# Sliding-window attention and an ELU feed-forward on one core: the order of the first four steps and of the last two products

## The chip, the core and the metric

The kernel runs on one core of a Trainium2 chip. A core has five engines that work side by side, each with an instruction queue of its own that it takes strictly in order, and wait for each other through semaphores: TensorE (PE in the profile; its weight loads are a row of their own, PEld), VectorE (DVE), ScalarE (ACT), GpSimd (POOL) and SyncE (SP). Data come from and go to the main memory by DMA, issued here from the queues of SP, ACT and POOL. Products of PE go to PSUM, and DVE or ACT take them from there into the core's working memory.

The metric is the time of one execution in microseconds (us) on the device. Lower is better.

## The reference: what is computed

Attention with a symmetric window over 8 batches, 8 heads, 576 positions and a head width of 64, and a feed-forward network on its result (4608 tokens by 512, 2048 hidden, ELU):

```
mask   = |pos_i - pos_j| <= 32
attn   = softmax(where(mask, q @ k.T / 8, -1e9))
x      = (attn @ v), heads side by side      # 4608 x 512
h      = x @ w_in                            # 4608 x 2048
g      = where(h > 0, h, exp(min(h, 0)) - 1)
out    = g @ w_out                           # 4608 x 512, float32
```

The inputs are float32; the products run in bfloat16 with float32 sums.

## The kernel before

**Attention.** Queries are taken in blocks of 64, two blocks (a pair) at a time; 36 pairs in all. For a pair, `scores` (L297) makes the transposed scores in PSUM, `exponential` (L312) takes them through ACT, `mask` (L319) multiplies by 0 and 1 on DVE, `pv` (L328) multiplies by the values and by a column of ones that gives the sums, `normalize` (L342) divides on DVE (a reciprocal and a product), `x_transpose` (L353) turns the result on PE and `x_evac` (L369) copies it to `xT`. A block of 64 queries needs 128 keys that start 32 before it. So values are loaded in two forms: `V_e[b]` holds blocks m of 128 positions that start at 128 m - 32, by `load_v` (L138), and `V_o[b]` holds the same rows shifted by 64, made from `V_e` by two copies of half the partitions each: `rotate_v` (L150) on DVE. Part 0 reads blocks m0 to m1 of `V_e`, part 1 the blocks one further on. Pairs 2 and 3 (blocks 4 to 7 of the first batch) use blocks 2 to 4 of the values, and so wait for the loads of values 3 and 4.

**Feed-forward.** Tokens go in tiles of 256 (two pairs), 18 tiles. The hidden width is worked in 8 steps of 256 columns per tile, 144 steps `kk`. A step is: the first product `mm1(kk)` (L591, 8 matmuls of 128x256 into PSUM `h0` or `h1` in turn), exp on ACT (e_sb), minus 1 (m_sb; on DVE, or on ACT for steps 1 to 3), `elu(kk)` (L623, one operation on DVE that joins the two cases and frees the PSUM tile), and the second product `mm2(kk)` (L635, 4 matmuls of 128x512: 2 halves of 128 rows by 2 blocks of the hidden width) that adds into the tile's output in PSUM. The first product of a step needs the tile's `xT` (both pairs); `order` (L586) makes steps 0 to 3 the first half of tile 0, steps 4 to 7 the first half of tile 1 (pairs 2 and 3), and then the second halves.

**Order.** It is written out by hand (`manual_schedule`): each engine gets its instructions in the order of the code. The loop at L661 runs for each kk: slot "first", `elu(kk-1)`, slot "dve", `mm1(kk)`, slot "mid", the due `mm2`, slot "end". `at(kk, slot, fn, ...)` puts pieces of attention into the slots. `mm2` follows two steps behind `mm1`, except at the start, where a small table delays products 0 to 3, and at the end, where 142 and 143 come after the last `mm1`. `idle(n, tag)` puts n matmuls on zeros into PE's queue.

The start, step by step: steps 0 and 1 need the first quarter of w_in, steps 2 and 3 the second, products 0 and 1 the first quarter of w_out. POOL's queue loads, with a cast to bfloat16: values 1, 0, 2; the second half of the first batch's q and k (`load_cast`); `load_w_in(0)`; three small operations on masks; `load_w_in(1)`; values 3 and 4; `load_w_out(0)` and `(1)`; then the next batch and the rest of the weights. Pairs 2 and 3 have scores and exponential behind step 0, masks around step 1, and rotation, `pv`, normalization and transpose in step 3, with products 0 and 1 between.

The end: `mm2(143)` is followed by two copies of 128x512 from PSUM, the first half's on DVE (written out from SP's queue), the last half's on ACT (from ACT's queue).

Of the kernel before, what the change touches and what calls it, by code (L numbers as in the profile page):

```python
# [9 lines left out]
FP32 = mybir.dt.float32  # L10
# [11 lines left out]
def kernel(  # L22
# [9 lines left out]
    nc = tc.nc  # L32
# [5 lines left out]
    D_MODEL = H * D  # L38
# [8 lines left out]
    VS = 5  # L47
# [7 lines left out]
    STEPS = NFO // FG  # L55
    HALF = STEPS // 2
    NSTEP = NT * STEPS
# [9 lines left out]
    opool = ctx.enter_context(tc.tile_pool(name="outs", bufs=2))  # L67
# [26 lines left out]
    def ps_tile(shape, dt, tag, name):  # L94
        return pools[tag].tile(shape, dt, tag=tag, name=name)
# [42 lines left out]
    def load_v(b, m):  # L138
        lo = 128 * m - WIN
        p0 = max(0, -lo)  # L140
        p1 = min(128, S - lo)
        nc.gpsimd.dma_start(  # L142
            out=V_e[b % 3][p0:p1, m, :, 0:D],
            in_=v[b, :, lo + p0:lo + p1, :].rearrange("h p d -> p h d"))
# [28 lines left out]
    def load_w_in(c):  # L173
        w = D_FF // 4
        nc.gpsimd.dma_start(  # L175
            out=w_in_sb[:, :, c * w:(c + 1) * w],
            in_=moe_w_in[:, c * w:(c + 1) * w].rearrange(
                "(o p) f -> p o f", p=128))

    def load_w_out(c):  # L180
        n = NFO // 4
        nc.gpsimd.dma_start(
            out=w_out_sb[:, c * n:(c + 1) * n, :],
            in_=moe_w_out[c * n * 128:(c + 1) * n * 128, :].rearrange(
                "(o p) f -> p o f", p=128))
# [46 lines left out]
    def copy_on(eng, d_, s_):  # L232
        if eng is nc.scalar:
            nc.scalar.copy(d_, s_)  # L234
        else:
            eng.tensor_copy(d_, s_)  # L236
# [169 lines left out]
    for mi in (0, 4):  # L406
# [4 lines left out]
        out=masks[:, 3, :], in_=masks[:, 3, :], compare_op=ALU.is_ge,  # L411
        fill=0.0, base=128 - WIN - 1, pattern=[[0, QB]],
        channel_multiplier=-1)
    load_w_in(1)
    for m in (3, 4):
        load_v(0, m)
    load_w_out(0)
    load_w_out(1)

# [49 lines left out]
    def at(kk, slot, fn, *args):  # L469
        tasks.setdefault((kk, slot), []).append((fn, args))  # L470

    def run(kk, slot):
        for fn, args in tasks.get((kk, slot), ()):
            fn(*args)
# [11 lines left out]
    at(0, "mid", scores, 3, "u")  # L486
    for i in (2, 3):
        at(0, "mid", exponential, i)
        at(1, "dve" if i == 2 else "mid", mask, i)
        at(3, "dve", rotate_v, 0, 2, VS - 1, (i - 2,))  # L490
        at(3, "mid", pv, i)

    at(1, "mid", idle, 3, "y1")
    at(3, "dve", idle, 3, "y1")
    for i in (2, 3):
        at(3, "mid", normalize, i)
    at(3, "mid", lambda: elu(2))
    for i in (2, 3):
        at(3, "mid", lambda n: mm2(n), i - 2)
        at(3, "mid", x_transpose, i)  # L500
        at(3, "mid", x_evac, i, nc.scalar)
    at(4, "dve", swap_pools)

    for part, kq in ((HALF_A, 7), (HALF_B, 15)):
# [20 lines left out]
    for i in range(4, NPAIR):  # L525
        two = i >= FIRST_TWO
        kk, z = begin[i], i % 2 if two else 0
# [5 lines left out]
        n = kk + (3 + z if two else 2)  # L533
# [55 lines left out]
    psH, m_t, g_t, psY = {}, {}, {}, {}  # L589

    def mm1(kk):  # L591
        t, s = order[kk]
        h = kk % 2


        tags = (f"h{h}", "s") if kk == NSTEP - 1 else (f"h{h}",)
        w = FG // len(tags)
        psH[kk], m_t[kk] = [], []
        for z, tag in enumerate(tags):
            ps = ps_tile([128, w, TT], FP32, tag, "ps")  # L600
            psH[kk].append(ps)
            for j in range(w):
                fo = s * FG + z * w + j
                for do in range(NDO):
                    nc.tensor.matmul(  # L605
                        ps[:, j, :],
                        lhsT=w_in_sb[:, do, fo * 128:(fo + 1) * 128],
                        rhs=xT[t][:, :, do, :],
                        start=(do == 0), stop=(do == NDO - 1))
        for z, ps in enumerate(psH[kk]):  # L610
            e_sb = mpool.tile([128, w, TT], FP32, tag="e_sb", name="e_sb")
            nc.scalar.activation(e_sb, ps, AX.Exp)  # L612
            m_sb = mpool.tile([128, w, TT], BF16, tag="m_sb", name="m_sb")
            if 1 <= kk <= 3:

                nc.scalar.activation(m_sb, e_sb, AX.Copy, bias=-1.0)
            else:
                nc.vector.tensor_scalar(m_sb, e_sb, -1.0, None, ALU.add)  # L618
            m_t[kk].append(m_sb)
            if kk == NSTEP - 1:  # L620
                elu(kk, z)

    def elu(kk, z=0):  # L623
        if z == 0:
            g_t[kk] = mpool.tile([128, FG, TT], BF16, tag="g_sb", name="g_sb",
                                   bufs=5)
        ps = psH[kk][z]
        w = ps.shape[1]
        nc.vector.scalar_tensor_tensor(  # L629
            g_t[kk][:, z * w:(z + 1) * w, :], ps, 0.0, m_t[kk][z],  # L630
            ALU.max, ALU.min)

    out_t = out.rearrange("(t ts p) c -> t p ts c", p=128, ts=TT // 128)

    def mm2(kk):  # L635
        t, s = order[kk]
        if s == 0:
            psY[t] = [ps_tile([128, D_MODEL], FP32, g, "psY")
                      for g in (("h2", "t0") if t == 1 else ("y0", "y1"))]
        g_sb = g_t.pop(kk)  # L640
        last = t == NT - 1 and s == STEPS - 1
        for ts in range(2):
            for j in range(FG):
                nc.tensor.matmul(  # L644
                    psY[t][ts],
                    lhsT=g_sb[:, j, ts * 128:(ts + 1) * 128],
                    rhs=w_out_sb[:, s * FG + j, :],
                    start=(s == 0 and j == 0),
                    stop=(s == STEPS - 1 and j == FG - 1))
        if s == STEPS - 1:  # L650
            for ts in range(2):
                z = 1 - ts if last else ts
                eng = (nc.scalar, nc.vector)[z]
                y_sb = opool.tile([128, D_MODEL], FP32, tag=f"y_sb{z}",
                                  name="y_sb")
                copy_on(eng, y_sb, psY[t][ts])
                (nc.scalar if last and ts else nc.sync).dma_start(
                    out_t[t, :, ts, :], y_sb)

    LAG = 2  # L660
    for kk in range(NSTEP + LAG):  # L661
        run(kk, "first")
        if 1 <= kk < NSTEP and kk != 3:
            elu(kk - 1)
        run(kk, "dve")
        if kk < NSTEP:
            mm1(kk)
        run(kk, "mid")

        for n in {2: (), 3: (), 4: (), 5: (2, 3)}.get(  # L670
                kk, (kk - LAG,) if kk >= LAG else ()):
            mm2(n)
        run(kk, "end")


# [28 lines left out]
```

## Time and profile before

| what | value |
|---|---|
| time, median of 3 runs (lowest, highest) | 306.71 us (306.45, 306.94) |
| the profiled execution: its time, its span | 306.45 us, 304.7 us |
| mean granted clock of TensorE | 1.000 |
| busy: PE, DVE, ACT, POOL | 294.7, 240.7, 170.3, 48.7 us |
| first products, L605: 1152 matmuls | 149.3 us, 273 ns each |
| second products, L644: 576 matmuls | 147.5 us, 379 ns each |
| starts of steps 0, 1, 2, 3, 4 on PE | 15.24, 16.80, 18.54, 20.69, 25.42 us |
| last matmul ends, last copy ends | about 300.40, 301.01 us |

The span runs from the first to the last instruction of the profiled execution; the time of the same execution is 1.75 us longer. A line of the timeline gives start and length in us, the engine, the line of the kernel (that of a helper, where one records the operation), the operation with what it writes and reads and the shape of one, how many are merged into the line, and in brackets how long the engine sat idle ahead of it and what ended that. Matmuls are pipelined: one is listed longer than the time after which the next starts. Line 236 is a copy or cast on DVE, 234 on ACT, whatever it copies. The view of windows gives, for stretches of time, the busy time of each engine, the granted clock, the mean busy share of the 16 DMA engines and the rate in GB/s.

### The profile page before, as it was taken

Reading aid. Unit: us, or ns where it says so; the run is one execution under the profiler, and the core shown is the slowest. Engines: PE = TensorE matmul, PEld = TensorE weight load, DVE = VectorE, ACT = ScalarE, POOL = GpSimd, SP = SyncE. Lnnn points to the kernel's source line nnn. Section 1 sums busy time; section 2 is a strip of 40 time slices with the busy share of each in tenths; the row PEclk is TensorE's granted clock in tenths of the full one; section 3 lists DMA queues with packets and bytes.
Section 4 is the critical chain, followed back from the end, with each engine's and each line's share of the span. In section 5 each row is a group of like instructions: output and inputs, shape, how many; then the busy total and the mean of one; then the engine's idle time right before and its main releaser. Section 6 shows DMA issues by size and latency. Waiting matters only on the chain.

```text
span 304.7 us, 7633 instructions
## 1 busy us (share of the span) xinstructions
PE 294.7 (97%) x3090; PEld 197.0 (65%) x3090; DVE 240.7 (79%) x470; ACT 170.3 (56%) x256; POOL 48.7 (16%) x68
## 2 busy tenths in 40 slices
PE   7799999999999999999999999999999999999994
PEld 3466666677666666666666666666666666666662
DVE  6866587978788887988798879887988787877663
ACT  3673556778664567546754675467545454543431
POOL 8836100910004100230023002300000000000000
PEclk9999999999999999999999999999999999999999
DMA  9999999999766997999799969996911111121011
GB/s 192 189 193 206 182 268 397 309 154 207 167 187 154 297 120 208 225 325 152 154 265 309 183 161 267 321 160 150 269 34 71 34 71 34 72 37 69 8 63 70
DMA packets 91973, 52.81 MB, mean 173 GB/s; under 512 B 76578, under 2 KB 81698, under 8 KB 91938
## 3 DMA queue, kind: packets, MB, share of 16 engines
q1 hardware_dynamic: 47186, 35.48, 43.6%
q0 software_dynamic: 42880, 10.10, 43.2%
q10 hardware_dynamic: 1872, 6.75, 5.7%
q8 instruction: 24, 0.39, 0.5%
q14 instruction: 11, 0.09, 0.1%
HBM read 36.70 MB, written 15.34 MB: 171 GB/s over the span
## 4 chain that ended last, share of the span: by engine, by line
PE 89%; DMA 4%; POOL 3%; DVE 1%; ACT 1%; issue 0%; POOLq 0%; DVEq 0%
PE psY L644 41%; PE ps L605 40%; DMA w_out_sb<-in_moe_w_out_dram 4%; PE psS L336 3%; PE psS L304 3%; POOL Ve L142 1%; PE ptx L279 1%; POOL c L136 1%; PE psXT L357 1%; POOL w_in_sb L175 0%; PE ptx L274 0%; ACT pu L315 0%; DVE x_st L348 0%; DVE pm L324 0%; DVE g_sb L629 0%
## 5 line engine op out<-in xcount | busy, mean ns | idle before, releaser
L612 ACT ACTIVATE e_sb<-ps 128x512 f32<-128x512 f32 (+1 forms) x145 | 86.3, 595 | 118.0 <-PE ps L605 110.4
L605 PE MATMUL ps<-xT,w_in_sb 128*128 128x256 bf16 x1152 | 149.3, 273 | 1.8 <-ACT xT L234 0.7
L644 PE MATMUL psY<-w_out_sb,g_sb 128*128 128x512 bf16 x576 | 147.5, 379 | 0.0
L605 PEld LDWEIGHTS <-w_in_sb 128*128 128x128 bf16 x1152 | 110.5, 98 | 40.7 <-DMA w_in_sb<-in_moe_w_in_dram 1.6
L629 DVE SCALAR_TENSOR_TENSOR g_sb<-ps,m_sb 128x512 bf16<-128x512 f32 (+1 forms) x145 | 99.4, 686 | 13.3 <-DVE m_sb L618 0.5
L618 DVE TENSOR_SCALAR m_sb<-e_sb 128x512 bf16<-128x512 f32 (+1 forms) x142 | 61.2, 431 | 38.3 <-ACT e_sb L612 36.4
L644 PEld LDWEIGHTS <-g_sb 128*128 128x128 bf16 x576 | 54.5, 98 | 38.5 <-DVE g_sb L629 0.2
L142 POOL DMA_DIRECT2D Ve<-in_v_dram x40 | 35.3, 893 | 138.9 <-PE psS L336 79.9
L315 ACT ACTIVATE pu<-psS 128x1024 bf16<-128x1024 f32 x36 | 36.5, 1021 | 1.4 <-PE psS L304 1.4
L348 DVE TENSOR_TENSOR x_st<-psS,rc 128x512 bf16<-128x512 f32 x36 | 24.9, 691 | 1.2
L324 DVE TENSOR_TENSOR pm<-pu,masks 128x1024 bf16<-128x1024 bf16 x36 | 24.6, 683 | 0.7 <-ACT pu L315 0.6
L234 ACT CAST qkb<-f 128x768 bf16<-128x768 f32 (+1 forms) x29 | 24.9, 860 | 0.0
L336 PEld LDWEIGHTS <-pm 128*64 128x64 bf16 x576 | 11.0, 111 | 8.8 <-DVE pm L324 7.7
L336 PE MATMUL psS<-Ve,pm 128*64 128x65 bf16 x320 | 13.2, 196 | 0.8 <-DVE pm L324 0.7
L236 DVE COPY y_sb<-psY 128x512 f32<-128x512 f32 x18 | 12.3, 684 | 0.9 <-PE psY L644 0.9
L304 PEld LDWEIGHTS <-kT 64*128 64x128 bf16 x576 | 9.6, 95 | 4.9 <-issue 4.0
L304 PE MATMUL psS<-qT,kT 64*128 64x64 bf16 x576 | 11.8, 191 | 0.5 <-DVE kT L236 0.5
L336 PE MATMUL psS<-Vo,pm 128*64 128x65 bf16 x256 | 11.9, 196 | 0.0
L234 ACT COPY y_sb<-psY 128x512 f32<-128x512 f32 x18 | 10.5, 582 | 2.2 <-PE psY L644 2.2
L153 DVE COPY Vo<-Ve 64x1040 bf16<-64x1040 bf16 x24 | 10.4, 435 | 1.3 <-DMA Ve<-in_v_dram 0.5
L395 PE MATMUL ps_idle<-zeros 128*128 128x512 bf16 x26 | 8.3, 450 | 1.3 <-DVE zeros L194 1.3
L234 ACT COPY qT<-ptx 128x1152 bf16<-128x1152 bf16 (+2 forms) x8 | 7.5, 972 | 3.5 <-PE ptx L279 2.8
(36 smaller groups left out, 73.3 us busy)
## 6 DMA issues: line engine op xcount, KB each, us to landing
out_dram<-y_sb SPq DMA_DIRECT2D x35, 256.0 KB, 3.7
f<-in_q_dram SPq DMA_DIRECT2D x12, 576.0 KB, 6.1
f<-in_k_dram SPq DMA_DIRECT2D x12, 576.0 KB, 8.2
in_dram<-qkb ACTq DMA_DIRECT2D x10, 576.0 KB, 4.5
Ve<-in_v_dram POOLq DMA_DIRECT2D x24, 128.0 KB, 11.4
w_in_sb<-in_moe_w_in_dram POOLq DMA_DIRECT2D x4, 512.0 KB, 9.8
w_out_sb<-in_moe_w_out_dram POOLq DMA_DIRECT2D x4, 512.0 KB, 12.5
Ve<-in_v_dram POOLq DMA_DIRECT2D x16, 96.0 KB, 10.3
```

The source lines that it names most:

```text
L142: nc.gpsimd.dma_start(out=V_e[b % 3][p0:p1, m, :, 0:D], in_=v[b, :, lo + p0:lo + p1, :].rearrange("h p d -> p h d"))
L234: nc.scalar.copy(d_, s_)
L304: nc.tensor.matmul(psS[:, h % 2, hp * 128 + z * QB:hp * 128 + (z + 1) * QB], lhsT=kT[b % 2][base:base + 64, KPAD + hp * S + QB * qb - WIN: ...
L315: nc.scalar.activation(pu, _bap(psS, [psS.ap[0], [1, 1024]]), AX.Exp, scale=SCALE)
L324: nc.vector.tensor_mul(pm, pu, _bap(mm, [mm.ap[0], [0, H], [1, 2 * QB]]))
L336: nc.tensor.matmul(psS[QB * z:QB * (z + 1), par, hp * VD:(hp + 1) * VD], lhsT=pm[:, par * HP + hp, z * QB:(z + 1) * QB], rhs=vv[:, qb // 2 ...
L348: nc.vector.tensor_mul(x_st, _bap(psS, [psS.ap[0], [VD, HP], [512, 2], [1, D]]), _bap(rc, [rc.ap[0], [2, HP], [1, 2], [0, D]]))
L605: nc.tensor.matmul(ps[:, j, :], lhsT=w_in_sb[:, do, fo * 128:(fo + 1) * 128], rhs=xT[t][:, :, do, :], start=(do == 0), stop=(do == NDO - 1))
L612: nc.scalar.activation(e_sb, ps, AX.Exp)
L618: nc.vector.tensor_scalar(m_sb, e_sb, -1.0, None, ALU.add)
L629: nc.vector.scalar_tensor_tensor(g_t[kk][:, z * w:(z + 1) * w, :], ps, 0.0, m_t[kk][z], ALU.max, ALU.min)
L644: nc.tensor.matmul(psY[t][ts], lhsT=g_sb[:, j, ts * 128:(ts + 1) * 128], rhs=w_out_sb[:, s * FG + j, :], start=(s == 0 and j == 0), stop=( ...
```

## The change

Three things are changed.

1. *Loads.* Values 3 and 4 stand ahead of w_in's second quarter in POOL's queue.
2. *Steps 0 to 3.* Rotations and masks of pairs 2 and 3 follow step 0 (rotation of part 0, mask 2, rotation of part 1, mask 3); both `pv` follow step 1, with 4, 2 and 1 idle matmuls around them (7, in place of 6 in two places); the normalizations stand ahead of step 2; the transposes follow step 3, with `elu(2)` in its usual place at the head of step 3, and products 0 and 1 behind both transposes. Minus 1 of steps 2 and 3 is on DVE.
3. *The end.* Products 142 and 143 run by halves of the rows: 142 and 143 on the first half, then both on the last. The first half is copied by DVE and sent by SP as before. The last half is copied by DVE and ACT, 256 columns each, and sent by SP and ACT.

```
-    load_w_in(1)
     for m in (3, 4):
         load_v(0, m)
+    load_w_in(1)
...
     for i in (2, 3):
         at(0, "mid", exponential, i)
-        at(1, "dve" if i == 2 else "mid", mask, i)
-        at(3, "dve", rotate_v, 0, 2, VS - 1, (i - 2,))
-        at(3, "mid", pv, i)
-
-    at(1, "mid", idle, 3, "y1")
-    at(3, "dve", idle, 3, "y1")
     for i in (2, 3):
-        at(3, "mid", normalize, i)
-    at(3, "mid", lambda: elu(2))
-    for i in (2, 3):
-        at(3, "mid", lambda n: mm2(n), i - 2)
+        at(0, "mid", rotate_v, 0, 2, VS - 1, (i - 2,))
+        at(0, "mid", mask, i)
+
+        at(1, "mid", idle, (4, 2)[i - 2], "y1")
+        at(1, "mid", pv, i)
+        at(2, "dve", normalize, i)
         at(3, "mid", x_transpose, i)
         at(3, "mid", x_evac, i, nc.scalar)
+    at(1, "end", idle, 1, "y1")
     at(4, "dve", swap_pools)
...
-            if 1 <= kk <= 3:
+            if kk == 1:
                 nc.scalar.activation(m_sb, e_sb, AX.Copy, bias=-1.0)
...
-    def mm2(kk):
+    def mm2(kk, parts=(0, 1)):
...
-        for ts in range(2):
+        for ts in parts:
             for j in range(FG):
                 nc.tensor.matmul(
                     psY[t][ts],
-                    lhsT=g_sb[:, j, ts * 128:(ts + 1) * 128],
+                    lhsT=g_t[kk][:, j, ts * 128:(ts + 1) * 128],
...
+        if last and s == STEPS - 1:
+            for ts in parts:
+                for z in range(1 + ts):
+                    c = slice(z * D_MODEL // 2 * ts,
+                              D_MODEL if z == ts else D_MODEL // 2)
+                    eng = (nc.vector, nc.scalar)[z]
+                    y_sb = opool.tile([128, D_MODEL], FP32,
+                                      tag=f"y_sb{1 - z}", name="y_sb")
+                    copy_on(eng, y_sb[:, c], psY[t][ts][:, c])
+                    (nc.scalar if z else nc.sync).dma_start(
+                        out_t[t, :, ts, c], y_sb[:, c])
...
-        if 1 <= kk < NSTEP and kk != 3:
+        if 1 <= kk < NSTEP:
             elu(kk - 1)
...
-        for n in {2: (), 3: (), 4: (), 5: (2, 3)}.get(
+        for n in {2: (), 3: (0, 1), 4: (), 5: (2, 3)}.get(
                 kk, (kk - LAG,) if kk >= LAG else ()):
-            mm2(n)
+            if n < NSTEP - 2:
+                mm2(n)
+            elif n == NSTEP - 1:
+                for ts in range(2):
+                    for m in (n - 1, n):
+                        mm2(m, (ts,))
```

More of the change, by code (lines that the diff above doesn't have):

```diff
@@ L639, in mm2 @@
                       for g in (("h2", "t0") if t == 1 else ("y0", "y1"))]
-        g_sb = g_t.pop(kk)
         last = t == NT - 1 and s == STEPS - 1
-        for ts in range(2):
+        for ts in parts:
             for j in range(FG):
@@ L649, in mm2 @@
                     stop=(s == STEPS - 1 and j == FG - 1))
-        if s == STEPS - 1:
+        if last and s == STEPS - 1:
[9 more added lines that the diff above has]
+                        out_t[t, :, ts, c], y_sb[:, c])
+        elif s == STEPS - 1:
             for ts in range(2):
-                z = 1 - ts if last else ts
-                eng = (nc.scalar, nc.vector)[z]
-                y_sb = opool.tile([128, D_MODEL], FP32, tag=f"y_sb{z}",
+                eng = (nc.scalar, nc.vector)[ts]
+                y_sb = opool.tile([128, D_MODEL], FP32, tag=f"y_sb{ts}",
                                   name="y_sb")
                 copy_on(eng, y_sb, psY[t][ts])
-                (nc.scalar if last and ts else nc.sync).dma_start(
-                    out_t[t, :, ts, :], y_sb)
+                nc.sync.dma_start(out_t[t, :, ts, :], y_sb)
     LAG = 2
```

## The prediction

> **What bounds the kernel now.** I read the page first: its engine table and the chain.
>
> ```profile
> PE 294.7 (97%) x3090; PEld 197.0 (65%) x3090; DVE 240.7 (79%) x470; ACT 170.3 (56%) x256; POOL 48.7 (16%) x68
> ...
> PE 89%; DMA 4%; POOL 3%; DVE 1%; ACT 1%; issue 0%; POOLq 0%; DVEq 0%
> ```
>
> TensorE (PE) is busy 97% of the span and is 89% of the chain. In the view of waits, PE's matmuls from 25 us on wait 0.7 us (for xT, at 25.42) and 0.2 us; its weight loads wait 6.5 us for pm, mostly while earlier matmuls still run. So from step 4 on PE runs almost without gaps, and a change earns time in two places only: ahead of step 4, where the chain is on DMA and POOL, and behind the last matmul. Whatever moves the start of step 4 moves everything behind it.
>
> Second view, the timeline of the first steps (start, length, engine, what ended the idle time):
>
> ```profile
> 16.96 0.43 DVE L618 TENSOR_SCALAR m_sb<-e_sb 128x512 bf16<-128x512 f32 x1 [2.04 <-ACT e_sb L612]
> ...
> 18.54 0.77 PEld L605 LDWEIGHTS <-w_in_sb 128*128 128x128 bf16 x8 [0.53 <-DMA w_in_sb<-in_moe_w_in_dram]
> ...
> 20.17 0.75 POOL L175 DMA_DIRECT2D w_in_sb<-in_moe_w_in_dram  x1 [0.86 <-DMA Ve<-in_v_dram]
> ...
> 20.67 0.93 DVE L153 COPY Vo<-Ve 64x1040 bf16<-64x1040 bf16 x2
> 20.69 1.03 PE L605 MATMUL ps<-xT,w_in_sb 128*128 128x256 bf16 x8 [0.46 <-DVE g_sb L629]
> ...
> 22.41 1.02 PE L644 MATMUL psY<-w_out_sb,g_sb 128*128 128x512 bf16 x4
> 22.42 0.69 DVE L348 TENSOR_TENSOR x_st<-psS,rc 128x512 bf16<-128x512 f32 x1
> ...
> 24.78 0.59 ACT L234 COPY xT<-psXT 128x512 bf16<-128x512 bf16 x1 [0.50 <-PE psXT L357]
> ...
> 25.42 1.91 PE L605 MATMUL ps<-xT,w_in_sb 128*128 128x256 bf16 x16 [0.67 <-ACT xT L234]
> ```
>
> Step 2 starts at 18.54 on w_in's second quarter; values 3 and 4 land behind it; their rotation, the attention of pairs 2 and 3 and two products follow, and step 4 starts at 25.42 on the last xT copy.
>
> Third view, the tail:
>
> ```profile
> 297.63 2.75 PE L644 MATMUL psY<-w_out_sb,g_sb 128*128 128x512 bf16 x12
> 298.98 0.42 DVE L629 SCALAR_TENSOR_TENSOR g_sb<-ps,m_sb 128x256 bf16<-128x256 f32 x1
> 299.99 0.69 DVE L236 COPY y_sb<-psY 128x512 f32<-128x512 f32 x1 [0.58 <-PE psY L644]
> 300.43 0.58 ACT L234 COPY y_sb<-psY 128x512 f32<-128x512 f32 x1 [2.21 <-PE psY L644]
> 301.04 0.36 ACTq L657 DMA_DIRECT2D out_dram<-y_sb  x1
> ...
> 301.60:301.80 0.20, 0.00 (x0) 0.00 (x0) 0.00 (x0) 0.00 (x0) 0.00 (x0) 1.00 0.97 358
> 302.80:303.00 0.20, 0.00 (x0) 0.00 (x0) 0.00 (x0) 0.00 (x0) 0.00 (x0) 1.00 0.70 246
> ```
>
> The last two lines are stretches of the span; their last columns are DMA share and GB/s. The rows of the last two writes go out from 301.5 to 303.1 without a gap. The DMA view has them landing 2.0 us after SP's issue at 300.71 and 2.7 us after ACT's at 301.04, so at 303.74; the span ends 0.96 later.
>
> **The loads.** Only the order on POOL's queue changes. By the DMA view, w_in(0) lands at 15.2, w_in(1) at 18.5, values 3 at 19.9, values 4 at 20.6, w_out(0) at 22.4, w_out(1) at 24.9: in the order of issue. With the values ahead, w_in(1) loses their 2.1 us and they gain what w_in(1) took: 3.3 us by its landing, or 512 KB at the 205 GB/s of the stretches around it, 2.5 us. So values 3 land at 16.6 to 17.3, values 4 at 17.3 to 18.1, w_in(1) at 20.0 to 20.6. The sum in front of w_out(0) is the same: 22.4. POOL's issues wait for the landing of the load eight issues earlier (15.73, 18.78, 20.17, each just behind one); two of them come up to 3 us sooner and queue behind all of these.
>
> **DVE after the change.** It gets, in program order: m(0), rotation 0, mask 2, rotation 1, mask 3, elu(0), elu(1), reciprocal and normalize of pairs 2 and 3, m(2), elu(2), m(3), elu(3). Pitches from the rows: a 0.69 us operation is followed by the next 0.60 to 0.64 later (two elu in 1.28), a rotation takes 0.465 (two in 0.93), reciprocal to normalize 0.25. From m(0) at 16.96: rotation 0 at 17.36; mask 2 at 17.88 (exponential 2 ends at 17.85); rotation 1 at 18.50; mask 3 at 18.96; elu(0) 19.58 to 20.27; elu(1) to 20.89; pair 2 normalized at 21.76, pair 3 at 22.60. The values have landed before each rotation, by 0.06 and 0.4 us at worst. m(2) and m(3), 0.43 each, move here from ACT (0.63 each there); they stand behind pair 3, and elu(3) is done at 24.9, ahead of the 25.6 at which step 5 wants its buffer. That cover is 0.7 us; beyond it each tenth on DVE costs a tenth.
>
> **PE after the change.** Four idle matmuls, pair 2 when rotation 1 ends (19.0), two idle, pair 3 when mask 3 ends (19.70), one idle: free at 20.27. Seven idles for six, all inside waits. Step 2 needs elu(0) (20.27, read by PE 0.05 later) and w_in(1) (20.0 to 20.6): 20.35. A step of 8 matmuls is 0.87 (16 in 1.74): step 3 at 21.22, done issuing at 22.09. Transpose of pair 2 at once; that of pair 3 waits for DVE at 22.60: matmuls at 22.76 (0.16 as from 23.11 to 23.27). Then product 0 at 22.99 (0.23 as from 23.27 to 23.50), 0.6 behind w_out(0); product 1 at 23.86; step 4 at 24.73. The xT copy of pair 3 ends near 24.0 on ACT, so the wait of 0.67 goes, and DVE's normalization of pair 3 is late in its place. Step 4: 25.42 to 24.73, a gain of 0.69. w_in(1) enters only if it lands after 20.67. Product 2 at 26.47 has w_out(1) 1.5 us before. Behind that everything shifts alike: w_in(2) lands at 30.4 or sooner, for step 8 near 34. I take 0.65, for small waits that I rounded off.
>
> **The tail.** The 12 last matmuls start 0.217 apart from 297.63. Now: product 141 (four), product 142 on the first half's rows (two, 298.50), product 143 on them: the first at 298.93, the second needs the elu that ends at 299.40. In the profile that matmul is the tenth, 299.58, its weights loaded at 299.46 right behind that elu; it is the eighth now and can't be earlier. So PE stands 0.43, the first half's copy starts at 299.99 as before, and the last matmul ends at 300.83 instead of 300.40: a loss of 0.43. The last copy is half as wide on each of two engines: from the 128x256 rows, 0.41 on ACT (two in 0.82) and 0.42 on DVE, for 0.58. Issue at 301.30 on both, for 301.04: 0.26 later. What that does to the end lies between two readings. By landing 2.0 us after issue, as the SP write did, it ends at 303.30: 0.44 gained. By the stretches, the first 256 KB move from 301.5 to 302.2, and the other 256 KB follow from there as now: nothing gained or lost. On the other side, rows of 1 KB (now 2 KB) are not in this trace; the slowest neighbour is the weight loads at 205 GB/s, which would make 1.25 us of the 0.7: a loss of 0.5. I take 0, nearest to the stretches, which show this very transfer bound by its rate.
>
> The Trainium skill speaks against this part of the change: "DMA: Bandwidth & Descriptors", section "Issuing engines are not separate DMA queues", says that transfers started by several engines run on the same 16 DMA engines and interleave, and that only sequencer time is saved. By that the tail's term is 0 or worse, and 0.44 by the landing row alone; both queues' rows inside one stretch at 0.97 of the 16 engines agree with it.
>
> **Sum.** -0.65 + 0 = -0.65: the profiled execution, 306.45 (span 304.7 and 1.75 around it), becomes 305.8. It is the lowest of the three runs; on their median, 306.71, the same difference gives 306.1.
>
> **The rivals.**
>
> *B, a wait takes the place of the other.* w_in(1) lands later than 20.67 because the values' small packets slow it; in the stretch 17.0 to 17.5, where they move, the rate is 162 GB/s for 205 and the DMA share nearly twice as high. From there step 4 moves one for one; landing at 21.3 leaves nothing: 306.7. Against it: everything lands 1.3 to 2.1 us behind its packets here, and w_out(0), first behind the values, came only 1.8 after them. The 0.5 of slower rows in the tail ends in the same place, 306.6. Together 0.20.
>
> *C, slower: DVE blocked by the values.* The rotations now stand in DVE's queue ahead of both masks, elu(0), elu(1) and everything that PE needs. If values 4 land after 18.5, all of it waits, one for one: 19.2 eats the gain, and landing at 20.2, nearly as before, gives step 4 at 26.4: 307.7. For it: the values' share of a queue is small, and a landing is counted when its slowest part is in. Against it: landings in the order of issue, all ten of them. 0.12.
>
> *D, the tail gains too:* the two halves land 2.0 us after issue: 305.6. 0.13. If the other way the half rows change nothing, that is my forecast.
>
> **How the numbers follow.** Forecast 306.1, 0.52; its own width is 305.8 to 306.4 from the pitches (0.05 on each of six DVE steps). B 0.20, C 0.12, D 0.13; 0.03 for losses I did not see. A measurement of this kernel tells about 0.2%, 0.61 us, from no change, so the line is at 306.1, where the forecast lies. Of its 0.52 I give 0.32 to faster and 0.20 to the same. Faster 0.32 + 0.13 = 0.45; same 0.20 + 0.20 = 0.40; slower 0.15. The range reaches from D's 305.6, with 0.2 for its spread, to B's 306.7 with the same: 305.4 to 306.9, and leaves out C.
>
> **What would show it.** Right: the rotations near 17.4 and 18.5 without a wait on DMA, step 2 on PE near 20.35, the transpose of pair 3 waiting on DVE, step 4 at 24.7, a PE wait of 0.4 for g_sb at 299 (all 0.7 earlier) and the last landing 2.4 us behind its issue. Wrong: a rotation that waits for Ve (C), step 2 waiting for w_in behind 20.7 (B), or gaps on PE between 25 and 60 us that were not there, which would mean that the gain is given back to a load.

## The result, and the profile after

The changed kernel takes 305.52 us in the median of 5 runs (305.43 to 306.17); the kernel before took 306.71 beside it (306.31 to 306.94). The ratio is 0.9969, with a 95% interval of 0.9955 to 0.9984, so it is faster by 0.3%, about 1 us (0.95 by the ratio, 1.19 between the two medians). The forecast was 306.1, a gain of 0.65, with a range of 305.4 to 306.9. Two later series, each beside the kernel before on one chip, gave 305.75 (ratio 0.9961, 0.9941 to 0.9980) and 305.34 (0.9967, 0.9956 to 0.9979).

The page of the kernel after, first its engine table and its chain:

```profile
PE 296.0 (97%) x3091; PEld 197.4 (65%) x3091; DVE 242.2 (80%) x473; ACT 168.6 (55%) x254; POOL 48.6 (16%) x68
...
PE 90%; DMA 3%; DVE 2%; POOL 2%; ACT 1%; issue 1%; DVEq 0%; POOLq 0%; ACTq 0%
```

DVE stands in the chain with 2% for 1%, POOL and DMA with 1% less each, as the change meant. The span of this execution is only 0.2 shorter than before (304.5 for 304.7; 306.17 with what lies around it, the longest of the five). Its timeline shows why:

```profile
16.17 1.05 PE L602 MATMUL ps<-xT,w_in_sb 128*128 128x256 bf16 x8 [1.37 <-DMA w_in_sb<-in_moe_w_in_dram]
...
17.88 0.43 DVE L615 TENSOR_SCALAR m_sb<-e_sb 128x512 bf16<-128x512 f32 x1 [2.79 <-ACT e_sb L609]
18.34 0.43 DVE L153 COPY Vo<-Ve 64x1040 bf16<-64x1040 bf16 x1
...
19.52 0.42 DVE L153 COPY Vo<-Ve 64x1040 bf16<-64x1040 bf16 x1
...
21.50 1.91 PE L602 MATMUL ps<-xT,w_in_sb 128*128 128x256 bf16 x16
...
22.86 0.69 DVE L348 TENSOR_TENSOR x_st<-psS,rc 128x512 bf16<-128x512 f32 x1
...
23.84 1.89 PE L640 MATMUL psY<-w_out_sb,g_sb 128*128 128x512 bf16 x8
...
25.57 1.69 PE L602 MATMUL ps<-xT,w_in_sb 128*128 128x256 bf16 x14
```

Step 0 started 0.93 later than before (16.17 for 15.24), because w_in's first quarter landed at 16.1. From there everything is shorter: step 0 to step 4 is 9.40 for 10.18. The rotations wait for nothing, steps 2 and 3 are one line of 16 matmuls, and behind pair 3's normalization (22.86 to 23.55) the products follow without a gap.

The last microseconds of the same kernel, the timeline and then the landing of its writes in the DMA view (KB, us from issue to landing):

```profile
297.79 1.67 PE L640 MATMUL psY<-w_out_sb,g_sb 128*128 128x512 bf16 x7
299.62 1.25 PE L640 MATMUL psY<-w_out_sb,g_sb 128*128 128x512 bf16 x5 [0.16 <-DVE g_sb L626]
300.05 0.69 DVE L236 COPY y_sb<-psY 128x512 f32<-128x512 f32 x1 [0.48 <-PE psY L640]
300.91 0.42 DVE L236 COPY y_sb<-psY 128x256 f32<-128x256 f32 x1 [0.17 <-PE psY L640]
301.37 0.37 ACT L234 COPY y_sb<-psY 128x256 f32<-128x256 f32 x1 [3.00 <-DVE y_sb L236]
301.77 0.36 ACTq L657 DMA_DIRECT2D out_dram<-y_sb  x1
```

```profile
out_dram<-y_sb SPq DMA_DIRECT2D x1, 128.0 KB, 1.8
out_dram<-y_sb ACTq DMA_DIRECT2D x1, 128.0 KB, 1.8
```

PE stands for the late elu, as worked out. ACT's half copy was expected beside DVE's; it waits until DVE's has ended. Even so the last write lands at 303.57, 5.78 behind the start of product 141; before it was 6.11 (303.74 less 297.63). That gain does not lie where the rows move. In stretches of 0.05 us, the steady stream of rows ends in the first of these lines in the kernel before, and in the second in the kernel after (last column: GB/s; in both the next stretch has 0, and one single row of the kernel before follows by 303.10):

```profile
302.95:303.00 0.05, 0.00 (x0) 0.00 (x0) 0.00 (x0) 0.00 (x0) 0.00 (x0) 1.00 0.33 82
303.10:303.15 0.05, 0.00 (x0) 0.00 (x0) 0.00 (x0) 0.00 (x0) 0.00 (x0) 1.00 0.28 82
```

That is 5.37 and 5.36 behind the start of product 141, so the rows are out at the same time. What shrank is the time from there to the last landing, 0.74 before and 0.42 after.

### The profile page after: what moved, and what is told of

Its sections match the earlier page's. It is cut to its first block, busy times and chain, and to the rows that moved or that the text cites. A ratio compares the mean times of both kernels' runs of the same rounds, so it can differ in the third digit from the quotient of the medians.

```text
span 304.5 us, 7644 instructions
## 1 busy us (share of the span) xinstructions
PE 296.0 (97%) x3091; PEld 197.4 (65%) x3091; DVE 242.2 (80%) x473; ACT 168.6 (55%) x254; POOL 48.6 (16%) x68
## 4 chain that ended last, share of the span: by engine, by line
PE 90%; DMA 3%; DVE 2%; POOL 2%; ACT 1%; issue 1%; DVEq 0%; POOLq 0%; ACTq 0%
PE ps L602 41%; PE psY L640 40%; PE psS L336 4%; PE psS L304 3%; DMA w_in_sb<-in_moe_w_in_dram 3%; PE ptx L279 1%; POOL Ve L142 1%; POOL c L136 1%; PE psXT L357 1%; DVE g_sb L626 1%; ACT pu L315 1%; DVE pm L324 0%; DVE m_sb L615 0%; PE ptx L274 0%; ACT e_sb L609 0%
## 5 line engine op out<-in xcount | busy, mean ns | idle before, releaser
L615 DVE TENSOR_SCALAR m_sb<-e_sb 128x512 bf16<-128x512 f32 x144 | 62.5, 434 | 38.3 <-ACT e_sb L609 36.5
L236 DVE COPY y_sb<-psY 128x512 f32<-128x512 f32 (+1 forms) x19 | 12.7, 671 | 1.0 <-PE psY L640 1.0
L234 ACT COPY y_sb<-psY 128x512 f32<-128x512 f32 (+1 forms) x18 | 10.3, 571 | 3.0 <-DVE y_sb L236 3.0
L395 PE MATMUL ps_idle<-zeros 128*128 128x512 bf16 x27 | 9.5, 482 | 1.3 <-DVE zeros L194 1.3
```

## The experiments

Three questions were open. Do the start and the end add up, or is one of them all of it? Was the late landing of w_in(0) chance (theory 1) or caused by the values that now stand behind it (theory 2)? And what gains at the end, where the forecast had nothing? "Start" is from step 0 to step 4, "tail" from the start of product 141 to the end of the span; where a matmul record is missing, product 141 is taken 272.21 behind step 4, as in the complete ones. The span is known to 0.1, so a tail is known to about 0.05. The ratio is to the kernel before in the same series, with its interval: 306.71 for the kernel after, 306.66 for start_only, tail_only, steps_old_loads and loads_old_steps, 306.69 for again, whole_copy, pair_order and own_bank, 306.53 for the other four.

| kernel | median | ratio | w_in(0): us to landing | start | tail |
|---|---|---|---|---|---|
| before | 306.71 | 1 | 7.7 | 10.18 | 7.07 |
| after | 305.52 | 0.9969 (0.9955 to 0.9984) | 8.4 | 9.40 | 6.71 |
| again | 305.75 | 0.9961 (0.9941 to 0.9980) | 7.4 | 9.47 | 6.71 |
| again_2 | 305.34 | 0.9967 (0.9956 to 0.9979) | 7.4 | 9.60 | 6.65 |
| start_only | 305.77 | 0.9979 (0.9966 to 0.9993) | 7.8 | 9.47 | 6.88 |
| start_only_2 | 305.86 | 0.9989 (0.9974 to 1.0004) | 7.5 | 9.38 | 7.01 |
| tail_only | 306.21 | 0.9987 (0.9979 to 0.9996) | 7.9 | 10.41 | 6.73 |
| steps_old_loads | 308.82 | 1.0067 (1.0042 to 1.0091) | 7.7 | 13.26 | 6.67 |
| loads_old_steps | 307.18 | 1.0011 (0.9997 to 1.0025) | | | |
| loads_old_steps_2 | 307.06 | 1.0018 (1.0009 to 1.0026) | 7.1 | 10.98 | 7.09 |
| whole_copy | 305.63 | 0.9960 (0.9937 to 0.9983) | 7.6 | 9.44 | 6.74 |
| pair_order | 305.68 | 0.9956 (0.9933 to 0.9978) | 7.3 | 9.66 | 6.83 |
| own_bank | 306.47 | 0.9988 (0.9969 to 1.0007) | 7.3 | 9.39 | 7.65 |
| own_bank_sp | 305.52 | 0.9969 (0.9959 to 0.9979) | 8.2 | 9.39 | 6.76 |

**The start alone.** The changed kernel with the end of the kernel before (`mm2` too is as before).

```
-            if n < NSTEP - 2:
-                mm2(n)
-            elif n == NSTEP - 1:
-                for ts in range(2):
-                    for m in (n - 1, n):
-                        mm2(m, (ts,))
+            mm2(n)
...
```

> The changed kernel with the old end (both halves of product 142 ahead of 143, one copy and one write per half); loads and steps 0 to 3 as changed. Theory 1 (the two parts add up, and w_in(0)'s late landing at 16.1 in the profile after is chance): step 0 at 15.2, step 4 0.78 sooner than before at 24.65, 305.9 in the median, 0.8 under the kernel before. Theory 2 (the values that now stand behind w_in(0) delay its landing by 0.9 in every execution): step 0 at 16.1, step 4 at 25.5, 306.7, no difference from before, and all that the change gains is in the end. Predicted on record for this part: 0.65 gained.

Measured: step 0 at 15.54, step 4 at 25.01, 305.77, 0.9 under the 306.66 of the kernel before beside it. Theory 1 expected 305.9. The start's gain is real, and w_in(0) landed 7.8 after its issue with the values behind it: against theory 2. (In start_only_2, further down, the median is 0.67 under the kernel before, but the interval of the ratio reaches 1.0004; one of its ten executions took 308.18 at a mean clock of 0.992.)

**The end alone.** The kernel before with the new `mm2` and the order by halves.

> The kernel before with the new end alone. Theory 1: from the first matmul of product 141 to the end of the span 6.71 us, as in the profile after, for 7.07: 0.36 gained, 306.35. Theory 2 needs the whole 1.2 here: 305.5. Predicted on record for this part: 0 (0.44 gained to 0.5 lost).

Measured: 306.21, 0.45 under the kernel before, with a tail of 6.73. So the forecast's 0 for the end does not hold, though 0.4 of a gain is near one of its two bounds.

**The values behind w_in(1), with the new steps.** This kernel is rival C of the prediction: the rotations stand early in DVE's queue, and the values land late.

```
+    load_w_in(1)
     for m in (3, 4):
         load_v(0, m)
-    load_w_in(1)
```

> The changed kernel with w_in's second quarter ahead of values 3 and 4 again, as before. Rival C of the prediction, put there on purpose: values land at 19.9 and 20.6, both rotations stand in DVE's queue ahead of the masks and elu(0), so rotation 0 starts at 19.95, pair 3 is normalized at 25.1 and step 4 starts near 27.3; 2.6 over the changed kernel, 308.1. If DVE's queue is not what sets step 4, the order of the loads makes less than 0.5 of difference to the changed kernel.

Measured: 308.82, 2.2 over the kernel before and about 3 over the changed one. The timeline of DVE and PE, and three stretches of the view of windows (third column from the end: the granted clock):

```profile
19.97 0.43 DVE L153 COPY Vo<-Ve 64x1040 bf16<-64x1040 bf16 x1 [2.37 <-DMA Ve<-in_v_dram]
...
21.18 0.22 PE L336 MATMUL psS<-Ve,pm 128*64 128x65 bf16 x1 [2.25 <-DVE pm L324]
...
23.19 3.52 PE L602 MATMUL ps<-xT,w_in_sb 128*128 128x256 bf16 x16
...
28.72 1.91 PE L602 MATMUL ps<-xT,w_in_sb 128*128 128x256 bf16 x16
```

```profile
22.00:23.00 1.00, 1.00 (x23) 0.53 (x20) 1.00 (x3) 0.00 (x0) 0.06 (x1) 1.00 1.23 205
23.00:24.00 1.00, 1.00 (x5) 0.62 (x5) 0.96 (x3) 0.00 (x0) 0.73 (x1) 0.53 1.21 202
25.00:26.00 1.00, 1.00 (x7) 0.69 (x6) 0.42 (x2) 0.60 (x1) 0.81 (x1) 0.50 1.25 217
```

The first rotation waits for the values until 19.97 (expected 19.95), and all of DVE's queue with it. Step 4 was expected near 27.3 and came at 28.72: PE had stood idle for 2.25 us until 21.18, and from 23.1 to 26.5 its granted clock was halved, so that the 16 matmuls of steps 2 and 3 took 3.52 for 1.91. Two of the seven executions kept a mean clock of 1.000; they took 307.46 and 307.54, and the others 308.65 to 310.55. So the blocked queue costs about 1.8 to 2.2 over the three medians of the changed kernel, which come from other series (2.6 were expected with the old loads' times). When the clock drops, it costs another 1.1 and more, which the prediction had not thought of.

**The loads alone.** The kernel before with only the two loads exchanged.

> The kernel before with values 3 and 4 ahead of w_in's second quarter, steps as before. Theory 1: step 2 waits for w_in(1) until about 20.4 in place of 18.54, step 3 starts near 22, the pairs behind it end later, step 4 near 26.5: 307.8, 1.1 over before; the order of the loads is worth something only with the new steps. If the order of the loads were the gain by itself: 305.9. Its profile also shows again where w_in(0) lands with the values behind it: 15.2 (chance) or 16.1 (theory 2).

> The kernel before with only the loads exchanged, again, since the profile of its first run was of a disturbed execution: step 2 on PE waits for w_in(1) until 20 to 20.6, step 3 starts near 21.5 to 22, step 4 at 25.9 to 26.5 if w_in(0) lands near 15.2, and 0.4 to 1.1 over the kernel before.

The profiled execution of the first run took 1065 us and says nothing of the others, so its columns are empty. Of the second run, two lines of PE's timeline:

```profile
19.73 1.05 PE L605 MATMUL ps<-xT,w_in_sb 128*128 128x256 bf16 x8 [1.57 <-DMA w_in_sb<-in_moe_w_in_dram]
...
25.89 1.91 PE L605 MATMUL ps<-xT,w_in_sb 128*128 128x256 bf16 x16 [0.67 <-ACT xT L234]
```

Step 2 waits for w_in(1), as expected, and the wait for xT at step 4 is still there. 307.06 is 0.5 over the kernel before, at the lower end of what was expected for this run; the first run's 307.18 is 0.5 over as well, where 1.1 was expected. So the order of the loads is a loss by itself (0.5) and the steps by themselves are one (2.2, the new end included); together they gain 0.7 to 0.9 (start_only_2 and start_only).

**The changed kernel again, twice.** No edit.

> The changed kernel as it is, once more, for a second profile and beside the next three on one chip. Theory 1: w_in(0) lands between 15.2 and 15.7, as in the four other profiles so far, step 4 at 24.7 to 25.1, and the median is 1.0 to 1.2 under the kernel before. Theory 2 (the values behind it delay w_in(0)): step 0 at 16.1 again.

> The changed kernel once more, beside start_only_2 on one chip, to settle what the new end adds. Theory 1 (start and end add up): 0.3 to 0.45 under start_only_2. Theory 3 (the end is worth no more than 0.1 once the start is changed; the 0.45 of tail_only was partly spread): within 0.2 of start_only_2.

Three lines of PE in the first of them, in place of 16.17, 21.50 and 25.57 above:

```profile
15.20 1.05 PE L602 MATMUL ps<-xT,w_in_sb 128*128 128x256 bf16 x8 [0.35 <-DMA w_in_sb<-in_moe_w_in_dram]
...
20.54 1.91 PE L602 MATMUL ps<-xT,w_in_sb 128*128 128x256 bf16 x16
...
24.67 1.58 PE L602 MATMUL ps<-xT,w_in_sb 128*128 128x256 bf16 x13
```

Theory 2 falls: with the values behind it w_in(0) lands 7.1 to 8.4 after its issue in ten profiles (median 7.45), with w_in(1) behind it 7.7 to 7.9 in three. The landing varies by up to 1.3 from one execution to the next, and the whole kernel moves with it: between the first two profiles of the changed kernel it is 1.0 sooner (7.4 for 8.4), and the profiled time is 0.9 shorter (305.26 for 306.17). How much of the spread between executions without a profile comes from it, no run shows.

> The changed kernel with the old end, again: 305.8 either way; what counts is the distance from again_2. In the profile, product 141 to the end of the span: 7.07 as before (theory 1) or about 6.7 as in its first profile (theory 3).

Measured: 305.34 for the changed kernel, 305.86 with the old end, on one chip: 0.5 apart in the medians, tails of 6.65 and 7.01. The four old ends have tails of 6.88 to 7.09 (mean 7.01), the five new ones 6.65 to 6.73 (mean 6.69): 0.32. Theory 3 falls, and start and end add up.

**Which part of the end.** First the order by halves with the old copies, then the old order with the split copies.

```
-                for z in range(1 + ts):
-                    c = slice(z * D_MODEL // 2 * ts,
-                              D_MODEL if z == ts else D_MODEL // 2)
+                for z in (ts,):
+                    c = slice(0, D_MODEL)
```

> The changed kernel, products 142 and 143 still by halves of the rows, but the last half copied whole by ACT and sent by ACT, as in the kernel before. If the split of the copy and of the write is what gains: the ACT write is issued 0.64 behind the last matmul (now 0.46 by SP and 0.88 by ACT) but lands 2.5 to 2.7 after its issue in place of 1.8: 0.4 over the changed kernel, no better than the old end. If the order of the products is what gains, no difference from the changed kernel.

```
-                for ts in range(2):
-                    for m in (n - 1, n):
-                        mm2(m, (ts,))
+                for m in (n - 1, n):
+                    mm2(m)
```

> The changed kernel with product 142 whole ahead of 143, as before, and the last half still copied and sent by two engines. By the prediction's working the products by halves lose 0.43 at the last matmul and gain nothing, since the first half ends with the late elu in either order. The last copies then wait for DVE's first copy (300.68), so 0.17 to 0.2 is won over the changed kernel: 305.4. If the halves were worth their stall: 0.2 or more over the changed kernel.

Measured: 305.63 and 305.68, tails of 6.74 and 6.83; the changed kernel beside them 305.75 and 6.71. The three can't be told apart. With the whole copy that is the second branch of what was expected: the split copy is not needed. With the old order the expectation misses: the stall of PE costs nothing (0.17 expected). Each half of the edit alone gives nearly all of the 0.3. What the two have in common is when ACT's last write is issued: 0.76 behind the first write of SP in the one, 0.74 in the other, 1.00 in the changed kernel, and 0.33 in the old end. In the one with the whole copy it is the very write of the old end, 256 KB by ACT. It is issued later than in the kernel before (3.74 behind product 141, for 3.41) and lands sooner (5.74 for 6.11):

```profile
out_dram<-y_sb SPq DMA_DIRECT2D x1, 256.0 KB, 2.0
out_dram<-y_sb ACTq DMA_DIRECT2D x1, 256.0 KB, 2.0
```

against 2.7 in the kernel before and 2.5 to 2.7 in the three others with the old end. That the spacing is the cause was not tested by an edit that moves it alone.

**Both waits of the end taken away.** Product 142 of the last half fills the stall, and the last 256 columns have a PSUM tile of their own.

```
+            if t == NT - 1:
+                psY[t].append(ps_tile([128, D_MODEL // 2], FP32, "u", "psYu"))
...
+                mm2(n - 1, (0,))
+                mm2(n, (0,), (0,))
+                mm2(n - 1, (1,))
+                mm2(n, (0,), (1,))
+                mm2(n, (1,))
```

> The changed kernel with two edits at its end: product 142 of the last half stands where PE stalled (order 142a, 143a first block, 142b, 143a second block, 143b), and the last 256 columns of the last half add up in a PSUM tile of their own, two matmuls of 256 columns for one of 512. If ACT's copy waited for DVE's (3.00 us idle, until y_sb of DVE) because both read one PSUM tile, ACT copies at once when the last matmul ends, 0.4 sooner, and writes 0.9 sooner than in the changed kernel; the writes are then bound by their rate, so 0.2 to 0.4 under the changed kernel: 305.2. If the wait has another reason, ACT still starts when DVE's half copy ends, and 0.1 to 0.2 is left.

Measured: both waits are gone, and it is slower, 306.47. ACT's copy starts at 299.59, on PE, with no wait for DVE, in the timeline of this kernel:

```profile
299.59 0.37 ACT L234 COPY y_sb<-psYu 128x256 f32<-128x256 f32 x1 [2.22 <-PE psYu L645]
299.87 0.81 SPq L663 DMA_DIRECT2D out_dram<-y_sb  x2
299.99 0.36 ACTq L663 DMA_DIRECT2D out_dram<-y_sb  x1
```

The DMA view has its two last writes land like this, and below it, for the next kernel, the one in which the only further edit is that ACT's half goes out by SP's queue (first the issues in its timeline, then the landing of the last two):

```profile
out_dram<-y_sb ACTq DMA_DIRECT2D x1, 128.0 KB, 2.3
out_dram<-y_sb SPq DMA_DIRECT2D x1, 128.0 KB, 3.2
```

```profile
300.65 1.30 SPq L663 DMA_DIRECT2D out_dram<-y_sb  x3
...
out_dram<-y_sb SPq DMA_DIRECT2D x2, 128.0 KB, 1.9
```

```
-                    (nc.scalar if z else nc.sync).dma_start(
+                    nc.sync.dma_start(
```

> The kernel own_bank with the ACT half of the last rows sent by SP's queue as well, behind the DVE half. In own_bank ACT copied at once, as expected, and its write was issued between the two of SP (299.99, between 299.87 and 300.3), but SP's second write then landed 3.2 us after its issue, for 1.8, and the kernel was 0.7 over the changed one. If ACT's write that comes in between is what holds SP's second write back: with one queue the last write lands 2 us after its issue near 300.6, and the kernel is at the changed one's 305.7 or up to 0.3 under it. If the extra matmuls and the third PSUM tile cost the time: 306.4 again.

Measured: 305.52, 0.95 under own_bank in the medians, tail 6.76 for 7.65. So neither the extra matmuls nor the third tile cost the time; ACT's write that was issued 0.12 behind SP's first did: SP's second write landed 3.2 after its issue. But the kernel with one queue is no faster than the changed kernel either (ratio 0.9969 for 0.9967). Its copies end 0.1 and 0.75 sooner, counted from product 141, but its writes are not issued sooner: SP's queue issues the three 0.43 and 0.48 apart, the last at 301.56, which is 4.02 behind product 141, for 3.98 in the changed kernel. No version that was run beats the changed kernel clearly.

## Why the prediction was right, and where not

**The bound.** Right. From step 4 to product 141 it is 272.21 before and 272.22 after, so what the start gains is kept to the end.

**The loads.** Right within its width: values 3 and 4 landed at 17.6 and 18.3, w_in(1) at 20.3 and w_out(0) at 22.8 in the execution whose w_in(0) was 0.9 late, still in the order of issue. What it left out is that w_in(0) itself varies by a microsecond, which the profile of one execution can't show.

**DVE and PE in the first steps.** Right to 0.1 at step 4 and to 0.2 on the way. In the second profile, whose w_in(0) landed as in the kernel before, the rotations start at 17.37 and 18.57 (forecast 17.36 and 18.50), step 2 at 20.54 (20.35), product 0 at 22.95 (22.99), step 4 at 24.67 (24.73). Two small errors cancel there. Pair 3's products began 0.22 behind mask 3's end (19.93 for 19.71), which the forecast had at nothing, so step 2 was 0.19 late; the wait of pair 3's transpose for DVE, which the forecast had behind it, took up the delay and was gone. Forecast was 0.69 for this part, and 0.65 was taken. The nine profiles with both the loads and the steps have a start of 9.38 to 9.66, mean 9.47, which is 0.71 under the 10.18 of before and 0.94 under the 10.41 of tail_only, the other profile with the old start. The two longest of the nine, again_2 and pair_order, have a second rotation of 0.63 and 0.70 us for 0.42; in both POOL was issuing a load meanwhile (from 18.15), but so it was during the end of the 0.42 in the second profile (from 18.72), so the cause stays open.

**The tail.** The mechanism of PE was right (the stall, the eighth matmul with the late elu), with sizes a little off: the eighth matmul started 0.31 late for 0.43 (299.62, where seven pitches of 0.217 behind 297.79 make 299.31), and the first half's copy started 0.1 sooner than before. The term of the tail was mis-sized: 0 was taken, 0.32 measured, between the taken value and the bound of 0.44. The step that failed is "I take 0, nearest to the stretches, which show this very transfer bound by its rate". Of the rows it was right: their stream ends 5.37 behind product 141 before and 5.36 after. But the end hangs on the landing, and the time from the last of the stream to the landing fell from 0.74 to 0.42. In the runs the last landing goes with the spacing of the two queues' writes: the tail is 0.2 to 0.3 shorter at 0.74 us of spacing and more than at 0.33, and longer at 0.12. Why is open.

"Issue at 301.30 on both" was wrong too: ACT waits for DVE, so its write went out at 301.61 on the time axis of the kernel before (301.77 less 0.16, by which product 141 started later). It landed 1.8 behind that, where the prediction's last part had 2.4 as the sign of being right, and its reading by the landing row 2.0. With a PSUM tile of its own the wait is gone. The Trainium skill, "PSUM — Partial Sum Buffer", section "PSUM bank collisions raise a hardware error", says that two engines may not touch one PSUM bank in the same rows at the same time, ACT beside DVE included. The trace agrees: ACT's copy starts at 301.37, released by DVE's, which runs from 300.91 to 301.33 (the 3.00 us on ACT's line are all of its idle time, most of it ahead of the last matmul). The prediction put the two copies side by side and priced no such wait. What the wait cost can't be read from the runs: where ACT's last write went out 0.24 sooner, with the whole copy, it carried 256 KB for 128, and the tail was no shorter (6.74 for 6.71).

**The rule weighed.** "Issuing engines are not separate DMA queues", of "DMA: Bandwidth & Descriptors" in the Trainium skill, gave 0 or worse for the tail. That a second queue brings no speed is borne out: one queue (6.76) is as good as two (6.71). "Or worse" came too, in the kernel whose two queues write 0.12 us apart: 3.2 us to landing, for 1.9 with one queue.

**The rivals.** B did not come: step 2 started at 20.54, and w_in(1) had landed at 20.4 (10.78 and 9.6 to landing). C did not come either, since the values were there; it is what happens with the loads in their old order, at 307.5 while the clock holds (307.7 was given for it) and 308.82 in the median with the clock's drop. D, the tail gaining, did come, with 0.32 for 0.44, beside a start that was right; so the sum is -0.71 - 0.32 = -1.03, and the ratio of 0.9969 makes -0.95. It came by another way than D's, though: the last issue was 0.31 later than D has it and the landing 0.2 sooner behind it, so that its time is near by luck. The range held the measured time because it reached down to D; the forecast itself, 0.65, was 0.3 short by the ratio.

## What to carry to other kernels

Two reorderings that are each a loss can be a gain together: a copy may only move up in an engine's strict queue if the load that it needs moves up first, else it holds back everything queued behind it. An engine's program order, written down with the pitches of the rows, forecast a rearranged start to 0.1 us at its end and 0.2 on the way. For transfers at the end of a kernel, read the landing and not only the rate at which rows move: here the rows were out at the same time, and the landing still differed by 0.3. And check whether two engines that are meant to read PSUM side by side read one tile: here the second waited for the first until it had a tile of its own.

## What the runs showed of the hardware that was not expected

In steps_old_loads a gap of 2.25 us on TensorE, with the small matmuls of two pairs and three idle ones behind it, was followed by a granted clock of one half for 3.4 us (0.50 in the stretch 23.2 to 26.4). The clock fell 1.9 us after the gap had ended. Five of the seven executions have a lower mean clock; the other two kept 1.000. The Trainium skill, "TensorE: Matmul & The Clock Gate", section "Part 1: The HAM clock gate", gives half the clock after at least one idle window of about 3.4 us and the full clock after a busy one, and has these windows run freely. The length of the slow stretch agrees; the gap here was shorter, and the measurement decides. The idle matmuls of this kernel are meant to prevent it: in the first and the second profile of the changed kernel the clock is 1.00 from 10 us to the last matmul. No run leaves them out, so that they do prevent it is not shown. The kernel before is not free of it either: 6 of its 90 executions beside these runs have a mean clock of 0.986 to 0.994 and took 307.45 to 309.44; none of them was profiled.

Two queues that write at once can end later than one: with ACT's 128 KB issued 0.12 us behind SP's 256 KB, SP's next 128 KB took 3.2 us to land, for 1.9 to 2.0 with one queue and 1.8 with ACT's write 1.00 behind. Why is open. The rate of the DMA engines was the same (about 310 to 380 GB/s in stretches of 0.2 us, in the second profile of the changed kernel too), and all but a few rows had gone out by 302.4, a microsecond ahead of the landing near 303.5. What differs between the profiles is the time from the end of the stream of rows to the last landing: 0.5 to 0.8 us in the four old ends, 1.2 in own_bank, 0.3 to 0.4 in all the others.
